# M in three groups a batch, batch 2's scores in the fixed banks, and another order of loads at the start

## The chip, the cores and the metric

The kernel runs on one core of a Trainium2 chip. A core has TensorE (PE; its weight loads are shown as PEld), VectorE (DVE), ScalarE (ACT), GpSimd (POOL) and SyncE (SP, which issues DMAs), an on-chip memory SBUF of 128 partitions, and PSUM, eight banks in which TensorE leaves its results. The metric is the time of one launch on the device in microseconds (us), lower is better, as a median of several runs.

## The reference

An attention block, and a feed-forward block behind it. B = 8 batches, H = 8 heads, S = 512 rows, Ns = 32 state rows, D = 64; then 8 x (512 + 32) = 4,352 rows of 512 pass through two weights with an ELU in between. All in fp32.

```
scores = x @ state.T / 8 ;  a  = softmax(scores)      # (S, Ns) for each batch and head
xread  = a @ state                                    # (S, D)
scores2 = state @ x.T / 8 ; a2 = softmax(scores2)     # (Ns, S)
sread  = a2 @ x
x_all  = concat(xread, sread) -> (B * 544, 512)
out    = elu(x_all @ w_in) @ w_out                    # w_in 512 x 2048, w_out 2048 x 512
```

## The kernel before

**M.** For x's rows the first product and the read are merged: `xread @ w_in = a @ (state @ w_in)`. The kernel makes M = state @ w_in for each batch (256 state rows, one set of 32 for each head, by 2,048 columns) and multiplies it with the transposed softmax, so w_in itself is used only for M and for the state rows at the end. M is made in half chunks `hc` of 256 columns, eight a batch, with small matmuls of 64 rows and 32 columns of the array (`by_state`), which fill two banks. `make_m` issues one or two half chunks as one operation of TensorE, `copy_m` brings the two banks to SBUF on ScalarE, and `sum_m` makes four block sums on GpSimd, for Strassen's scheme (seven block products in place of eight).

**Stages of a batch.** From batch 2 on a batch has a first half, `batch`: four chunks of 512 columns of g = elu(a @ M), each of seven products `two` in two parts, which use two ordinary banks (`pa`, `pc`) and a fixed one (`pb`); and a second half, `ffn2` (`ffn2_1` for batch 1): g @ w_out by two nested Strassen levels. There, each of the second-level products `second[k]` has seven steps of four matmuls in two banks. The next batch's scores, softmax, block sums of the softmax (`sum_a`), first M groups and state read are woven into this second half. Before the change M comes in four groups a batch: half chunks (0, 1) and (2, 3) in the second half of the batch before, (4, 5) and (6, 7) between the chunks of `batch`. The half chunks of w_in come from a copy in DRAM (`w_in_mem`) by `fetch`, into three slots of `w_half` (slot `hc % 3`).

**The start.** `start` loads states, x of batches 0 and 1 and the weights. Weights are converted by ScalarE and VectorE after loading (`convert`, sixteen blocks of 1 MB: eight of w_in, eight of w_out). `w_step` converts a block of w_in and makes M from it for batches 0 and 1. At the end of `start` stand batch 0's second half and the scores of batch 2. The operations of the loads have a `rank`, which sets their order on the DMA queue. In the first 40 us, where TensorE is planned to have nothing to do, `fill` matmuls (shown at L1590) keep it busy.

**What sets the order.** All operations are first collected in a `Plan`. A list scheduler with a cost for each operation (`Plan.run`) then fixes each engine's order before the program is built: TensorE takes operations in the order they were written if they are ready, the others by due times worked back from TensorE's, GpSimd and the DMAs as given. It also gives out the eight PSUM banks. Two of them, 6 and 7, are `fixed`: an operation that opens one takes just this one, and from the first such operation on the others share the remaining six. Before the change each fixed bank is opened by a product that serves only this, `ident_ready` (L1137), after batch 0's second half; the scores of batches 3 to 7 reuse those banks, batch 2's scores take two ordinary ones. `Plan.behind(op)` makes all operations collected inside it, except GpSimd's, wait for `op`.

`m_to` says where M of each chunk lies:

```python
m_to = {0: m_sb[:, 0], 1: m_sb[:, 1], 2: s_buf, 3: m_sb[:, 0]}
```

`s_buf` is also the place of a Strassen operand (`o.s`) in the second half. Nearly all instructions are issued by one helper, so their line is L464 throughout, and they are told apart by their tiles: `ps<-w_half,kT` is an M group, `ps<-aT,m` and `ps<-aT,s` are chunks, `ps<-w_out,g`, `ps<-sec`, `ps<-t_w,s` and the like are steps of the second half, `ps<-o,kT` and `ps<-xr,kT` are scores.

Of the kernel before, what the change touches and what calls it, by code (L numbers as in the profile page):

```python
# [86 lines left out]
class Plan:  # L87
# [108 lines left out]
    def prepare(self):  # L196
        for op in self.ops:
            op.users = []
            op.turn = self.places.get(op.number, op.number)
        for op in self.ops:  # L200
            for d in op.deps:
                d.users.append(op)
        self.opening = {}
        self.closing = {}
        for b in self.banks:
            self.opening.setdefault(b.first, []).append(b)
            self.closing.setdefault(b.last, []).append(b)
        self.kept = {b.first: b.fixed for b in self.fixed}
        self.all_banks = min([op.number for op in self.kept], default=0)
# [29 lines left out]
    def run(self, until=0.0):  # L239
# [9 lines left out]
        fixed = set(self.kept.values())  # L249
# [9 lines left out]
        def bank_time(op):  # L259

            if op in self.kept:
                return min([t for t, i in banks if i == self.kept[op]], default=None)
# [45 lines left out]
        while len(done) < len(self.ops):  # L308
# [26 lines left out]
            if op in self.kept:  # L335
                banks = [b for b in banks if b[1] != self.kept[op]]
                if self.kept[op] in holder:
                    after.append((holder[self.kept[op]], op))
# [51 lines left out]
def kernel(  # L390
# [297 lines left out]

    def m_blocks(m):
# [26 lines left out]
    def sum_a():  # L716
# [3 lines left out]
        (V if 0 else Q).tensor_tensor(out=t1, in0=r12, in1=r11, op=ALU.subtract)  # L720
        (V if 0 else Q).tensor_tensor(out=t2, in0=r22, in1=t1, op=ALU.subtract)
        (V if 0 else Q).tensor_tensor(out=r12, in0=r22, in1=r12, op=ALU.subtract)
        (V if 0 else Q).tensor_tensor(out=t4, in0=r21, in1=t2, op=ALU.subtract)
# [36 lines left out]
    def softmax(b, to):  # L760
# [15 lines left out]
        line(b, total_t, 1.0, eps)  # L776
        V.reciprocal(out=total_t, in_=total_t)
        for g in range(G):
            (V if 0 & 2 and b > 1 or b in [] else Q).tensor_tensor(
# [161 lines left out]
    class Second:  # L941
# [39 lines left out]
        def steps(self, out, fresh=False, base=None):  # L981
# [3 lines left out]
            x, y = bank(), bank()  # L985
            steps = []

            def step(n, ps, a, b, first, last, h, c):
# [10 lines left out]
                )  # L999
                o, p = (x[:, h, c * P : (c + 1) * P] for x in (out, base or out))  # L1000
                if n not in (0, 2, 3, 6):
# [10 lines left out]
            for n, args in enumerate((  # L1012
                (x, a11, self.b11, True, False, 0, 0),
                (y, a12, self.b21, True, True, 0, 0),
                (x, s[2], t[2], False, False, 1, 0),
                (y, s[3], t[3], True, False, 1, 1),
                (x, s[1], t[1], False, False, 1, 1),
                (y, a22, t[4], False, True, 1, 0),
                (x, s[4], self.b22, False, True, 0, 1),
            )):  # L1020
                steps.append(lambda n=n, args=args: step(n, *args))
# [128 lines left out]
    def start():  # L1150
# [22 lines left out]
        load_states(0, 1, raw_s, (SP, ACT))  # L1173
        load_x(0, x_halves, (SP, ACT))
        blocks[0] = weight_block(0, 2)
        load_states(1, 2, raw_s[:, 1:], (SP,))
        load_x(1, x_1)
        read_block(1)
        read_block(2)
# [4 lines left out]
        def w_step(hc):  # L1184
            convert_block(hc)
# [16 lines left out]
        turn_x(x_halves, ob, 1)  # L1202
        scores(0, ob)
        softmax(0, a_sb)
        w_step(0)
        ffn1(0, 0, (0, 1), 0 & 1)
        turn_x(x_1, ob)
        scores(1, ob)
        softmax(1, aT1)
        ffn1(1, 0, (0, 1), 0 & 2)  # L1210
        w_step(1)
        ffn1(0, 0, (2, 3))
        ffn1(1, 0, (2, 3))
        for c in range(1, 4):
# [3 lines left out]
            if c < 2:  # L1218
                for b in range(2):
                    softmax_rows(b)  # L1220
# [39 lines left out]
        scores(2, xr)  # L1260
# [14 lines left out]
    def first_m(b, at=None):  # L1275
# [7 lines left out]
        fetch(3)  # L1283

    def ffn2(o, b):
# [4 lines left out]
        o.sum_1()  # L1290
        late = [plan.ops[-1]]
        if 0:
            second[1].sums(o.a11, spare + s_2[0][:1])
            steps = second[1].steps(c12, fresh=True)
# [6 lines left out]
        if nxt:  # L1301
            first_m(b + 1, 1)
            scores(b + 1, xr, [f.view() for f in fixed])
        else:
            turn_read()
        for f in steps[1:]:
            f()
        second[2].sums(o.a12, s_2[1] + spaces(a_sb))
        late.append(plan.ops[-1])
        for f in second[2].steps(c11, base=c12):  # L1310
            f()
        late.append(plan.ops[-1])
        second[4].sums(o.a22, s_2[0] + spare[:2])
        late.append(plan.ops[-1])
        for f in second[4].steps(c21, fresh=True):
            f()
        second[6].sums(o.s, s_2[1] + spaces(a_sb))
# [11 lines left out]
        def soft_next():  # L1329
            if nxt:  # L1330
                with plan.behind(late[4]):
# [23 lines left out]
        if nxt:  # L1355
            make_m(b + 1, 2, 3)
            copy_m(b + 1, 1, m_to[1])
            sum_m(m_to[1])
            state_read(b + 1)
# [4 lines left out]
    def ffn2_1(o, b, x1):  # L1364
# [31 lines left out]
        make_m(b + 1, 2, 3)  # L1396
        copy_m(b + 1, 1, m_to[1])
        sum_m(m_to[1])
        state_read(b + 1)
# [34 lines left out]
    def batch(b):  # L1434
        for hc in range(4, 7):
# [8 lines left out]
        p[1] = ffn1_chunk(b, 1, g_sb)  # L1444
        p[0][1]()
        make_m(b, 4, 5)
        fetch(7)
        copy_m(b, 2, m_to[2])
        sum_m(m_to[2])
        p[1][0]()  # L1450
        p[2] = ffn1_chunk(b, 2, g_sb)
        p[1][1]()
        make_m(b, 6, 7)
        copy_m(b, 3, m_to[3])
        sum_m(m_to[3])
# [124 lines left out]
    ident_ready(0)  # L1580
    ident_ready(1)
# [50 lines left out]
```

## Time and profile before

| | |
|---|---|
| median of 3 runs | 702.73 us (702.24 to 704.44) |
| the profiled execution, on the device | 704.65 us |
| its span, first to last instruction | 702.9 us |
| mean granted TensorE clock | 0.997 |
| ACT, POOL busy (share of the span) | 43%, 21% |
| moved by DMA | 78.55 MB, 112 GB/s on average |
| matmul records of M groups (`ps<-w_half,kT`) | 1024, of 5794 on TensorE |

A row of the timeline gives the start in us, the length, engine, line, operation, the tiles it writes and reads (out<-in), the shape, and how many instructions were merged into it; in brackets, the idle time before it and what ended it. Matmuls overlap in the pipeline, so the length of a row is longer than the time until the next can start; the distance of two starts is the better measure. Every fp32 matmul call leaves two records. A row of the windows gives a stretch, its length, and the busy time of each engine in it with the number of instructions, then the granted clock, the DMA share and GB/s.

### The profile page before, as it was taken

To read this page: it belongs to the slowest core of one execution; us is meant where nothing else is said; L and a number is where in the kernel's file an instruction comes from. 1 tells how busy PE (TensorE), PEld (TensorE's weight loads), DVE (VectorE), ACT (ScalarE), POOL (GpSimd) and SP (SyncE) were. 2 spreads that over 40 slices of the span, in tenths; PEclk is the share of its full clock that TensorE was granted. 3 is DMA by queue.
4 is the path that set the end of the run, shared out by engine and by line. 5 is a ranking of instruction groups with operands and counts; after the bars stand their busy time and mean duration, and the time that the engine had idled before them with its cause. 6 is when DMAs were issued, how large, how long until landed. Compare 5 with 4: busy or idle time off the path is not lost.

```text
span 702.9 us, 14562 instructions
## 1 busy us (share of the span) xinstructions
PE 692.8 (99%) x5794; PEld 591.0 (84%) x5794; DVE 563.8 (80%) x991; ACT 303.9 (43%) x628; POOL 144.2 (21%) x161
## 2 busy tenths in 40 slices
PE   8899999999999999999999999999999999999997
PEld 7544468889988998889988998899888997899996
DVE  4899999999649985899669985998589966997650
ACT  4899982011148122742176215712373227500530
POOL 1300000052211062303530181116220453000000
PEclk9999999999999999999999999999999999999999
DMA  8578774204262505740471417450565034200300
GB/s 213 189 261 274 239 249 73 61 31 120 71 140 92 121 11 152 171 115 8 120 182 56 95 29 194 108 122 14 153 165 121 1 120 152 61 1 31 121 8 23
DMA packets 111268, 78.55 MB, mean 112 GB/s; under 512 B 89184, under 2 KB 92768, under 8 KB 111200
## 3 DMA queue, kind: packets, MB, share of 16 engines
q1 hardware_dynamic: 108988, 77.06, 39.4%
q8 instruction: 46, 0.75, 0.4%
q10 hardware_dynamic: 2212, 0.56, 0.4%
q14 instruction: 22, 0.18, 0.1%
HBM read 61.34 MB, written 13.11 MB: 106 GB/s over the span
## 4 chain that ended last, share of the span: by engine, by line
PE 94%; ACT 2%; DMA 2%; DVE 1%; SPq 1%; issue 0%; ACTq 0%; DVEq 0%
PE ps L464 93%; DMA g<-in_x_dram 1%; DMA xe<-in_x_dram 1%; SPq L464 1%; DVE w_half L464 1%; ACT sec L464 1%; ACT w_half L464 0%; ACT t_w L464 0%; PE ps L1590 0%; ACT m L464 0%; DVE sec L464 0%; DVE t_w L464 0%; ACTq L464 0%; DVE g L464 0%; ACT g L464 0%
## 5 line engine op out<-in xcount | busy, mean ns | idle before, releaser
L464 PE MATMUL ps<-aT,m 128*128 128x256 f32 (+1 forms) x568 | 149.7, 407 | 0.4 <-ACT m L464 0.4
L464 PE MATMUL ps<-w_out,g 128*128 128x128 f32 (+1 forms) x864 | 144.2, 315 | 0.0
L464 PEld LDWEIGHTS ps<-w_out,g 128*128 128x128 f32 x864 | 126.1, 191 | 14.9 <-issue 4.2
L464 PEld LDWEIGHTS ps<-aT,m 128*128 128x128 f32 x568 | 104.8, 190 | 33.3 <-issue 15.1
L464 DVE TENSOR_TENSOR o<-o,ps 128x128 f32<-128x128 f32 (+2 forms) x239 | 68.8, 289 | 66.9 <-PE ps L464 66.2
L464 ACT COPY o<-ps 128x128 f32<-128x128 f32 (+2 forms) x70 | 23.2, 335 | 158.7 <-PE ps L464 152.7
L464 POOL TENSOR_TENSOR xr<-xr,small 128x512 f32<-128x512 f32 x24 | 30.9, 1306 | 290.5 <-PE ps L464 147.1
L464 POOL TENSOR_TENSOR m<-m 128x256 f32<-128x256 f32 x72 | 63.6, 907 | 52.0 <-ACT m L464 50.6
L464 PE MATMUL ps<-sec 128*128 128x128 f32 x560 | 74.1, 275 | 0.0
L464 PEld LDWEIGHTS ps<-sec 128*128 128x128 f32 x560 | 68.5, 192 | 0.7 <-issue 0.4
L464 PE MATMUL ps<-t_w,s 128*128 128x128 f32 (+1 forms) x432 | 64.9, 298 | 0.0
L464 ACT ACTIVATE xe<-ps 128x512 f32<-128x512 f32 x96 | 54.4, 599 | 20.4 <-PE ps L464 15.0
L464 PEld LDWEIGHTS ps<-t_w,s 128*128 128x128 f32 x432 | 58.6, 192 | 3.3 <-ACT m L464 0.8
L464 ACT COPY m<-ps 128x512 f32<-128x512 f32 (+1 forms) x56 | 26.8, 535 | 55.6 <-PE ps L464 55.6
L464 DVE TENSOR_TENSOR ps<-sec,ps 128x512 f32<-128x512 f32 (+1 forms) x52 | 34.6, 673 | 17.5 <-PE ps L464 15.4
L464 DVE SCALAR_TENSOR_TENSOR g<-xe,ps 128x512 f32<-128x512 f32 x66 | 43.3, 684 | 1.7 <-ACT xe L464 1.1
L464 ACT COPY ps<-ps 128x512 f32<-128x512 f32 (+1 forms) x28 | 15.1, 541 | 61.2 <-PE ps L464 61.2
L464 ACT COPY sec<-ps 128x512 f32<-128x512 f32 (+1 forms) x52 | 29.7, 571 | 26.6 <-PE ps L464 18.5
L464 PE MATMUL ps<-aT,s 128*128 128x256 f32 x168 | 41.0, 379 | 0.0
L464 ACT ACTIVATE xe<-xe 128x512 f32<-128x512 f32 x66 | 38.8, 636 | 0.4
L464 PE MATMUL ps<-w_half,kT 64*32 64x256 f32 x1024 | 35.8, 382 | 0.6 <-DVE w_half L464 0.4
L464 PEld LDWEIGHTS ps<-aT,s 128*128 128x128 f32 x168 | 31.8, 190 | 4.5 <-DVE ps L464 0.2
(151 smaller groups left out, 1146.5 us busy)
## 6 DMA issues: line engine op xcount, KB each, us to landing
w_half<-w_in_mem SPq DMA_DIRECT2D x54, 512.0 KB
t_w<-in_moe_w_out_dram SPq DMA_DIRECT2D x8, 1024.0 KB
t_w<-in_moe_w_in_dram SPq DMA_DIRECT2D x7, 1024.0 KB
out_dram<-o SPq DMA_DIRECT2D x14, 512.0 KB
xe<-in_x_dram SPq DMA_DIRECT2D x26, 256.0 KB
o<-in_x_dram SPq DMA_DIRECT2D x80, 64.0 KB
w_in_mem<-w_half SPq DMA_DIRECT2D x8, 512.0 KB
xr<-xr SPq DMA_DIRECT2D x96, 32.0 KB
```

The costliest lines, as they stand in the source:

```text
L464: ins = getattr(engine, name)(**named)
```

## The change

Six edits come together.

1. **Three groups of M.** `make_three(b, pair, one)` makes three half chunks as one operation on TensorE: the pair into two banks as before, the single one into two more. `copy_one` copies the single half chunk into its place in M. A batch now has the groups (0, 1), (2, 3, 4) and (6, 7, 5). The second stands where (2, 3) stood, with a dependence on the first step of the second-level product before it. The third stands where (4, 5) stood. The sums of chunk 2 and chunk 3 both follow it.
2. **Fetches.** `first_m` fetches half chunk 4 as well; `batch` begins with 5, 6, 7 in place of 4, 5, 6 and fetches nothing later.
3. **Batch 2's scores in the fixed banks.** They become the operation that opens banks 6 and 7, both at once, which `Plan` learns to handle; the two `ident_ready` products go.
4. **Order of loads at the start.** The first block of w_in is ranked ahead of batch 0's x, and the second block ahead of batch 1's x; the third comes last. The order of the other work there, written as a string now, stays as it was.
5. **VectorE in place of GpSimd.** The last product of the softmax (times the reciprocal of the sum) for batches 0 and 1, and the four sums of `sum_a` in every batch that has them.
6. **The next batch's softmax** in `ffn2` waits for `late[3]` (the last sum of `second[4]`) in place of `late[4]` (that of `second[6]`).

Other variants in the diff are switched off by constants (`if 0`, `via = 0`, `sl = 0`, `fm = 0`) and are cut here.

```diff
-        self.kept = {b.first: b.fixed for b in self.fixed}
+        self.kept = {}
+        for b in self.fixed:
+            self.kept.setdefault(b.first, []).append(b.fixed)
...
             if op in self.kept:
-                return min([t for t, i in banks if i == self.kept[op]], default=None)
+                free = [t for t, i in banks if i in self.kept[op]]
+                return max(free) if len(free) == len(self.kept[op]) else None
...
+    def make_three(b, pair, one):
+
+        c = pair[0] // 2
+        ps = st[b, "m", c] = [bank(), bank()]
+        half = st[b, "m", one] = [bank(), bank()]
+        calls = []
+        for hc in (*pair, one):
+            w, h = st["w", hc], hc % 2
+            calls.append(by_state(
+                b, half if hc == one else ps, [w[:, m] for m in range(NP)],
+                slice(0, 256) if hc == one else slice(h * 256, (h + 1) * 256), hc == one or h == 0,
+            ))
...
+            products(1.38, sum(calls, []), "make_m", "state")
+
+    def copy_one(b, hc, to):
+        for g in range(G):
+            A.copy(
+                out=to[:, g * 512 + hc % 2 * 256 :][:, :256], in_=st[b, "m", hc][g][:, :256],
+            )
+        g_of[b, hc // 2] = to
...
-        (V if 0 else Q).tensor_tensor(out=t1, in0=r12, in1=r11, op=ALU.subtract)
+        (V if 1 else Q).tensor_tensor(out=t1, in0=r12, in1=r11, op=ALU.subtract)
...
-            (V if 0 & 2 and b > 1 or b in [] else Q).tensor_tensor(
+            (V if 0 & 2 and b > 1 or b in [0, 1] else Q).tensor_tensor(
                 out=rows(g), in0=rows(g), in1=bc(tops(b, g)["total_t"], NS), op=ALU.mult
             )
...
-        load_states(0, 1, raw_s, (SP, ACT))
-        load_x(0, x_halves, (SP, ACT))
-        blocks[0] = weight_block(0, 2)
-        load_states(1, 2, raw_s[:, 1:], (SP,))
-        load_x(1, x_1)
-        read_block(1)
-        read_block(2)
+        q2 = (SP, ACT)
+        for what in 'swxtvyu':
+            if what == "s": load_states(0, 1, raw_s, q2)
+            if what == "x": load_x(0, x_halves, q2)
+            if what == "w": blocks[0] = weight_block(0, 2)
+            if what == "t": load_states(1, 2, raw_s[:, 1:], (SP,))
+            if what == "y": load_x(1, x_1)
+            if what == "v": read_block(1)
+            if what == "u": read_block(2)
...
-        scores(2, xr)
+        scores(2, xr, [f.view() for f in fixed] if 1 else None)
...
         fetch(2)
         fetch(3)
+        if 1: fetch(4)
+
+    def next_m(b):
...
+            before = [op for op in plan.ops if op.name == "second"][-7]
+            make_three(b, (2, 3), 4)
+            plan.ops[-1].deps.add(before)
...
+        copy_m(b, 1, m_to[1])
+        if 1: copy_one(b, 4, m_to[2])
+        sum_m(m_to[1])
+        if not 0:
+            state_read(b)
...
-                with plan.behind(late[4]):
+                with plan.behind(late[3]):
...
-        for hc in range(4, 7):
+        for hc in range(5, 8) if 1 else range(4, 7):
             fetch(hc)
...
+        def m_three():
+            make_three(b, (6, 7), 5)
+            copy_one(b, 5, m_to[2])
+            copy_m(b, 3, m_to[3])
+            sum_m(m_to[2])
+            sum_m(m_to[3])
...
+        mm = 3
         p[0][1]()
-        make_m(b, 4, 5)
-        fetch(7)
-        copy_m(b, 2, m_to[2])
-        sum_m(m_to[2])
+        if mm == 0: m_2()
+        if mm == 1: m_both()
+        if mm == 3: m_three()
         p[1][0]()
...
         p[1][1]()
-        make_m(b, 6, 7)
-        copy_m(b, 3, m_to[3])
-        sum_m(m_to[3])
+        if mm == 0: m_3()
...
-    ident_ready(0)
-    ident_ready(1)
+    if not 1:
+        ident_ready(0)
+        ident_ready(1)
     ffn2_1(o, 1, x1)
```

## The prediction

> **What bounds the kernel now.** I read the page's first row (busy time), then the chain that ended last, then the row of granted clock.
>
> ```profile
> PE 692.8 (99%) x5794; PEld 591.0 (84%) x5794; DVE 563.8 (80%) x991; ACT 303.9 (43%) x628; POOL 144.2 (21%) x161
> ...
> PE 94%; ACT 2%; DMA 2%; DVE 1%; SPq 1%; issue 0%; ACTq 0%; DVEq 0%
> ```
>
> TensorE is busy 99% of 702.9 us and is 94% of the chain. A modelled busy time proves little by itself, so I look at the distance between starts in the timeline, which is the rate at which work really leaves.
>
> ```profile
> 335.13 1.06 PE L464 MATMUL ps<-t_w,s 128*128 128x128 f32 x8
> 336.12 1.09 PE L464 MATMUL ps<-w_half,kT 64*32 64x256 f32 x32
> 337.14 1.16 PE L464 MATMUL ps<-w_out,g 128*128 128x128 f32 x8
> 338.14 1.06 PE L464 MATMUL ps<-sec 128*128 128x128 f32 x8
> 339.03 1.06 PE L464 MATMUL ps<-t_w,s 128*128 128x128 f32 x8
> ```
>
> A product of eight records (two for each matmul call) takes 0.89 us from start to start (338.14 to 339.03) wherever one follows another, in all batches. So from about 36 us on TensorE streams without holes, and **a microsecond less of its instructions is a microsecond less of time**, as long as its suppliers keep up. The exceptions are the edges of an M group (the 64*32 row): the product before it takes 0.99 (335.13 to 336.12), the one after it 1.00.
>
> **The M groups.** What has one group less? Groups of one, two and three half chunks all occur in the trace:
>
> ```profile
> 68.42 0.66 PE L464 MATMUL ps<-w_half,kT 64*32 64x256 f32 x16
> 69.01 5.42 PE L464 MATMUL ps<-aT,m 128*128 128x512 f32 x12
> ...
> 81.23 1.53 PE L464 MATMUL ps<-w_half,kT 64*32 64x256 f32 x48
> 82.68 7.13 PE L464 MATMUL ps<-aT,m 128*128 128x512 f32 x16
> ```
>
> Start to next start is 0.59 for one half chunk (x16), 1.02 for two (x32, above), 1.45 for three (x48): 0.15 fixed and 0.43 for each half chunk. With the edges, 0.10 and 0.11, a group costs 0.36 whatever it holds. The matmuls are as many as before, so each batch from 2 to 7 saves one 0.36: **6 x 0.36 = 2.1 us**.
>
> [...] The row: copies of M on ScalarE have a median of 586 ns at 128x512 and a shortest of 354 ns at 128x256, so a group of three needs 2 x 0.59 + 2 x 0.35 = 1.9 us of copies behind 1.45 of matmuls. It holds four banks, of the six that are not fixed. Six of the twelve new groups, one in each batch, stand between two chunks: two banks chunk 0, four M, none left for chunk 1. By the rule chunk 1 waits until the copies end: 1.9 + 0.2 of delay, less the 0.86 of chunk 0's last product, 1.2 us. The other six stand beside a second-level product that already holds its two banks for seven products; taking 1.2 there too gives 12 x 1.2 = +14 us. By the rows, M copies start 0.16 after a group ends (355.49 to 355.65, group at 354.47) with ScalarE idle for 0.49 before, a half bank is free 0.35 later, and chunk 1 needs one bank first and the second 0.86 later: 0. I take 0, nearer to that row, and keep both ends.
>
> **Hidden parts of the same edit.** Fetches stay eight a batch. 5, 6 and 7 must now all land before one group. SP's queue issues 16 moves of attention rows until 344.76 and then two fetches at 344.86; a third there is 9 us ahead of the place of the old group (354.47). If it stays where it is (356.42, behind two stores and four block loads) the group slips to the old last group's place (361.85), still ahead of chunk 2. Cost 0; without that cover up to some 5 us. Six pairs of sums on GpSimd run back to back (2.92 us each, 21% busy), before chunk 2's second product: 0. ScalarE has two more copies a batch, at 43% load: 0.
>
> **The two readiness products.**
>
> ```profile
> 160.61 1.95 PE L464 MATMUL ps<-w_out 128*128 128x128 f32 x16
> 162.39 1.95 PE L464 MATMUL ps<-t_w,s 128*128 128x128 f32 x16
> ```
>
> They read weights twice, feed nothing, and occupy 160.61 to 162.39: **1.8 us less**, same shape as what follows, so no edge goes. What is late next is VectorE: the sum read by TensorE's `sec` product at 165.30 runs at 162.36 for 0.69 and ends at 163.05. Slack 2.2 us, of which 1.8 is eaten. Batch 2's scores (at 138.76) now wait for banks 6 and 7 both; their result is first used at 197.76, so even 20 us of delay are covered: 0.
>
> **Sums of the attention on VectorE.** GpSimd loses 24 of 0.95 us; VectorE gets 24 of 128x256 at 0.42 (its nearest row with that shape), 1.7 us a batch, in this stage (columns: stretch, length, then busy time of PE, PEld, DVE, ACT, POOL):
>
> ```profile
> 331.00:337.00 6.00, 6.00 (x79) 5.49 (x77) 5.35 (x13) 0.67 (x3) 5.75 (x7) 1.00 0.06 15
> 337.00:343.00 6.00, 6.00 (x60) 5.86 (x53) 4.41 (x8) 1.07 (x2) 5.92 (x7) 1.00 0.20 53
> ```
>
> VectorE's idle 0.65 + 1.59 holds it. Below: no gain, since no TensorE wait there names GpSimd. Above: all of it delays the evacuations behind it on VectorE, 6 x 1.7 = 10 us. I take 0. Softmax tied to an earlier sum (`late[3]`): the same instructions one product earlier; 0, at most 0.3 each way for five batches.
>
> **The start.**
>
> ```profile
> 10.94 1.09 PE L464 MATMUL ps<-o,kT 64*32 64x512 f32 x16 [0.27 <-DVE o L464]
> ...
> 19.09 2.29 POOL L464 TENSOR_TENSOR sec<-sec 128x512 f32<-128x512 f32 x2 [2.96 <-DVE sec L464]
> ...
> 25.08 0.70 DVE L464 STREAM_TRANSPOSE aT<-sec 128x512 f32<-128x512 f32 x1
> ...
> 26.54 3.60 PE L464 MATMUL ps<-aT,m 128*128 128x512 f32 x8
> ...
> 29.97 1.05 PE L1590 MATMUL ps<-sec 128*128 128x128 f32 x8
> ...
> 35.45 3.70 PE L464 MATMUL ps<-aT,m 128*128 128x512 f32 x8 [0.36 <-ACT m L464]
> ```
>
> Block 0 is 1.05 MB; the DMA row moves 332 to 379 GB/s when weights go, so x comes up to 3.0 us later and scores start at 13.9, not 10.94. From the first transpose (12.11) to the reciprocal's end (19.01) is 6.9; then two products on VectorE (0.6 apart by its 128x512 rows) and two transposes (0.7) make 2.7 with nothing between, where now the second transpose ends at 25.78. Ready: 12.1 + 3.0 + 9.6 = 24.7, **1.1 earlier**; block 0's conversion, which M waited for at 25.21, fits into the wait for x. But batch 1's x comes behind block 1, 3.0 later; its softmax runs from 23.27 to 38.08 on a VectorE that is busy nearly throughout and gets 4 x 0.6 more. Head start (conversion of block 0 from about 8 instead of 11.45), 3, against 3.0 of later data and 2.4 of added work that only partly collide. I take **-0.5**, range -3 to +2.
>
> [...] The trace's longest TensorE gap between 15 and 20 us is under 1 us, yet the clock granted in 20 to 25 is 0.68, and batch 1's scores take 1.89 from start to start where batch 0's took 1.02. [...] by the row one more such window over 128x512 products costs up to 1.7, and one less gives back 0.9. I take 0.
>
> **Sum.** -2.1 - 1.8 - 0.5 = -4.4. On the profiled execution: span 702.9 to 698.5, its time 704.65 (1.75 around the span) to 700.2. The median of the runs shown is 702.73, 1.9 below that execution; I forecast the median: **698.3**.
>
> **Rivals.** (1) *The start gives more*: if VectorE's head start counts in full, the hole of 29.97 to 35.45 closes by half, -3 in place of -0.5: 695.8. For it: that hole waits for M, hence for block 1, which now comes 3 us earlier. Against: batch 1's later x. (2) *VectorE is the bound between 40 and 180 us*: it is 8.8 to 10 of every 10 us there. Then the 1.8 turn into waiting at the `sec` product, the start is lost too, and only the groups stay, with some 0.6 given back: 701.2. Against: TensorE waits for VectorE hardly anywhere now, and batch 2's softmax can be put off. (3) *Slower: bank starvation.* The four banks of a group of three stop TensorE at the next bank it opens, at both places of each batch. At 1.2 us for each of 12 groups: 702.7 - 3.9 + 14.4 = 713. It decides from 0.5 us a group on (6.0 / 12). For it: 2 + 4 = 6 banks exactly; against: the copies' prompt start. (4) *The group isn't merged*: M's half chunk waits for its fetch or banks and other products come between; then 2.1 is lost, 700.4, part of rival 2's range.
>
> **How the numbers follow.** 0.3% is 2.1 us, about what this measurement can tell. Forecast 0.60 (696.3 to 700.3, all faster); rival 1 0.15 (faster); rivals 2 and 4 0.18, one third faster; rival 3 0.07 (slower). Faster 0.81, same 0.12, slower 0.07. The range 695.0 to 701.6 leaves a tenth at each end.
>
> **What would show it.** Right: three 64*32 rows a batch, two of x48 with 1.45 to the next start, and products of 0.89 right after; no `ps<-w_out` row near 160; batch period 75.8 (260.32 to 336.12) down to 75.4. Wrong: TensorE rows that wait for ACT `m` or `s` behind an x48 row (rival 3), for DVE `sec` near 161 (rival 2), or the first 128x512 products later than 26.5.

## The result, and the profile after

| | before | after |
|---|---|---|
| median | 702.62 us (702.24 to 704.44, 4 runs) | 696.89 us (696.14 to 697.11, 4 runs) |
| the profiled execution, span | 702.9 us | 695.1 us |
| ratio, 95% interval | | 0.9912 (0.9893 to 0.993) |

The forecast was 698.3, range 695.0 to 701.6. The page of after, first its row of busy time, then the row of the chain that ended last:

```profile
PE 684.7 (98%) x5782; PEld 590.5 (85%) x5782; DVE 572.4 (82%) x1019; ACT 302.2 (43%) x640; POOL 112.7 (16%) x133
...
PE 90%; ACT 4%; DMA 4%; DVE 1%; issue 1%; ACTq 0%
```

TensorE is still the bound: its busy time went down by 8.1 us, the span by 7.8. VectorE's rose by 8.6 us, from 80 to 82%, and GpSimd's fell by 31.5. The helper's line is now L466. The timeline of after, TensorE alone, shows the second and, further down, the first M group of a batch (batch 3's group of three, batch 4's group of two):

```profile
254.95 1.53 PE L466 MATMUL ps<-w_half,kT 64*32 64x256 f32 x48
256.41 1.16 PE L466 MATMUL ps<-sec 128*128 128x128 f32 x8
257.40 1.06 PE L466 MATMUL ps<-t_w,s 128*128 128x128 f32 x8
...
301.29 1.09 PE L466 MATMUL ps<-w_half,kT 64*32 64x256 f32 x32
```

The x48 row takes 1.46 to the next start, the edge behind it 0.99 for a product of 0.89. The first group of a batch starts at 226.08, 301.29, 376.50 and 451.71: a period of **75.21**, where the same rows of before are 75.79 apart (231.44, 307.24, 383.03, 458.82).

Around 160 us, the same view:

```profile
156.67 1.95 PE L466 MATMUL ps<-t_w,s 128*128 128x128 f32 x16
158.55 1.09 PE L466 MATMUL ps<-xr,kT 64*32 64x512 f32 x16
```

No `ps<-w_out` row stands ahead of `ps<-t_w,s` any more; batch 2's scores run behind it.

**Where the 5.7 us came from.** The two traces can be laid side by side at rows that both have. But before's first profiled execution was granted a clock of only 0.68 in 20 to 25 us. A second profile of before (next section) has a span of 701.4 and no such stretch, so I count against that one. The two traces differ by 6.3 us, the medians by 5.7; the parts below are parts of the 6.3.

| row | before, second profile | after | lead, and what it gained since the row above |
|---|---|---|---|
| first `ps<-t_w,s` of 128x256 | 123.47 | 122.14 | 1.33 (start) |
| `ps<-t_w,s` of 128x128 x16 | 161.00 | 156.67 | 4.33: 1.78 from the readiness products, 1.22 is only lent, as batch 2's scores are still to come |
| first M group of batch 3 | 230.05 | 226.08 | 3.97: the loan is paid back, 0.86 was gained in batch 2 |
| first M group of batches 4 to 7 | 305.83, 381.63, 457.43, 533.22 | 301.29, 376.50, 451.71, 527.51 | 4.54, 5.13, 5.72, 5.71 |
| end of TensorE's work | 696.73 | 690.42 | 6.31 |

So: start 1.33, readiness products 1.78, and 3.20 in the six batches 2 to 7, one of which (up to the row at 527.51) gained nothing. From the distances of starts, the 3.20 are 2.16 for six groups less (6 x 0.36), 1.19 of short waits between the products of the chunks and 0.44 of two waits for VectorE's sums at 166.79 and 167.92, which before has and after has not, less 0.59 for a standstill that only after has (batch 6).

### The profile page after: what moved, and what is told of

Same layout as the page of the kernel before. It is cut to its first block, busy times and chain, and to the rows that moved or that the text cites. A ratio compares the mean times of both kernels' runs of the same rounds, so it can differ in the third digit from the quotient of the medians.

```text
span 695.1 us, 14567 instructions
## 1 busy us (share of the span) xinstructions
PE 684.7 (98%) x5782; PEld 590.5 (85%) x5782; DVE 572.4 (82%) x1019; ACT 302.2 (43%) x640; POOL 112.7 (16%) x133
## 4 chain that ended last, share of the span: by engine, by line
PE 90%; ACT 4%; DMA 4%; DVE 1%; issue 1%; ACTq 0%
PE ps L466 90%; ACT sec L466 2%; DMA xe<-in_x_dram 1%; DMA t_w<-in_moe_w_out_dram 1%; DMA g<-in_x_dram 1%; ACT t_w L466 1%; DVE w_half L466 0%; ACT o L466 0%; DVE t_w L466 0%; DVE sec L466 0%; ACT w_half L466 0%; ACTq L466 0%; ACT g L466 0%; ACT m L466 0%; ACT s L466 0%
## 5 line engine op out<-in xcount | busy, mean ns | idle before, releaser
L466 PE MATMUL ps<-aT,m 128*128 128x256 f32 (+1 forms) x568 | 147.9, 405 | 0.2
L466 PE MATMUL ps<-w_out,g 128*128 128x128 f32 (+1 forms) x864 | 144.2, 314 | 0.0
L466 PEld LDWEIGHTS ps<-w_out,g 128*128 128x128 f32 x864 | 126.3, 191 | 12.4 <-issue 4.2
L466 PEld LDWEIGHTS ps<-aT,m 128*128 128x128 f32 x568 | 106.2, 190 | 29.6 <-issue 14.1
L466 DVE TENSOR_TENSOR o<-o,ps 128x128 f32<-128x128 f32 (+2 forms) x239 | 67.3, 286 | 41.2 <-PE ps L466 40.5
L466 ACT COPY o<-ps 128x128 f32<-128x128 f32 (+2 forms) x70 | 23.1, 335 | 145.6 <-PE ps L466 139.6
L466 POOL TENSOR_TENSOR xr<-xr,small 128x512 f32<-128x512 f32 x24 | 30.0, 1271 | 335.1 <-DVE small L466 171.3
L466 PE MATMUL ps<-sec 128*128 128x128 f32 x560 | 74.8, 277 | 0.0
L466 PEld LDWEIGHTS ps<-sec 128*128 128x128 f32 x560 | 68.5, 192 | 4.0 <-DVE o L466 3.7
L466 POOL TENSOR_TENSOR m<-m 128x256 f32<-128x256 f32 x72 | 60.5, 861 | 27.1 <-ACT m L466 25.7
L466 PE MATMUL ps<-t_w,s 128*128 128x128 f32 (+1 forms) x432 | 64.5, 298 | 0.0
L466 ACT ACTIVATE xe<-ps 128x512 f32<-128x512 f32 x96 | 54.9, 602 | 19.4 <-PE ps L466 12.8
L466 PEld LDWEIGHTS ps<-t_w,s 128*128 128x128 f32 x432 | 58.6, 192 | 2.5
L466 ACT COPY m<-ps 128x512 f32<-128x512 f32 (+1 forms) x56 | 28.1, 540 | 61.0 <-PE ps L466 60.9
L466 DVE SCALAR_TENSOR_TENSOR g<-xe,ps 128x512 f32<-128x512 f32 x66 | 43.9, 682 | 9.8 <-DMA w_half<-w_in_mem 5.8
L466 DVE TENSOR_TENSOR ps<-sec,ps 128x512 f32<-128x512 f32 (+1 forms) x52 | 34.9, 671 | 14.1 <-ACT sec L466 7.2
L466 ACT COPY sec<-ps 128x512 f32<-128x512 f32 (+1 forms) x52 | 29.7, 571 | 28.6 <-PE ps L466 28.5
L466 PE MATMUL ps<-aT,s 128*128 128x256 f32 x168 | 41.2, 379 | 0.0
L466 ACT ACTIVATE xe<-xe 128x512 f32<-128x512 f32 x66 | 39.8, 636 | 0.7
L466 PEld LDWEIGHTS ps<-aT,s 128*128 128x128 f32 x168 | 31.9, 190 | 4.3
L466 PE MATMUL ps<-w_half,kT 64*32 64x256 f32 x1024 | 34.9, 381 | 0.7 <-DVE xe L466 0.4
L466 PE MATMUL ps<-sec,g 128*128 128x128 f32 (+1 forms) x252 | 31.5, 272 | 1.2 <-DMA g<-in_x_dram 1.2
```

The source lines that it names most:

```text
L466: ins = getattr(engine, name)(**named)
```

## The experiments

Ratios are to the kernel before. After's is 0.9912, uncertain by 0.0018, that is by some 1.3 us, so the traces decide on the parts, at the rows of the table above ("the row at 122" is the first `ps<-t_w,s` of 128x256).

### The kernel before once more

No edit.

> The kernel before once more, unchanged, with a new profile. Question: does the window of half clock at 19.74 us (granted clock 0.68 in 20 to 25 us, batch 1's scores 1.89 us from start to start) belong to this kernel or to that one execution? Theory A (it belongs to that execution alone): the clock is 1.0 in 20 to 25 us, batch 1's scores take 1.02 us, the first product of w_out starts at 94.5 to 95.0 instead of 96.52, and the span is 700.5 to 701.5. Theory B (it belongs to the kernel, because its products wait longer near 15 to 20 us): the window comes again, the scores take 1.9, the first product of w_out is at 96.5 and the span is 702.5 to 703.

Ratio 0.9995 (0.9986 to 1.0005), span 701.4. Theory A. The windows and the timeline of this second profile of before:

```profile
20.00:25.00 5.00, 4.74 (x120) 2.76 (x120) 4.91 (x9) 4.76 (x12) 1.84 (x3) 1.00 0.47 149
```

```profile
24.74 3.60 PE L464 MATMUL ps<-aT,m 128*128 128x512 f32 x8
28.17 1.05 PE L1590 MATMUL ps<-sec 128*128 128x128 f32 x8
...
37.19 7.03 PE L464 MATMUL ps<-s,g 128*128 128x512 f32 x16
```

The eighth figure, the granted clock, is 1.00, and batch 1's scores take 1.02 (20.29 to 21.31). The same program, in the same order, was once given half a clock for a while and once not. That execution's 1.4 us at the row near 122 (124.86 against 123.47) belong to no edit.

### Four groups again

```diff
-        if 1: fetch(4)
+        if 0: fetch(4)
...
-        if 1:
+        if 0:
             before = [op for op in plan.ops if op.name == "second"][-7]
             make_three(b, (2, 3), 4)
...
-        if 1: copy_one(b, 4, m_to[2])
+        if 0: copy_one(b, 4, m_to[2])
...
-        for hc in range(5, 8) if 1 else range(4, 7):
+        for hc in range(5, 8) if 0 else range(4, 7):
...
-        mm = 3
+        mm = 0
```

> The changed kernel with M again in four groups a batch (two of x48 become one x32 and two pairs as before; the fetches of w_in as before), all other edits kept. Theory A (a group costs what stands around it and the short wait behind a group of two, 0.22 us a batch): 6 x 0.58 = 3.5 us, less the one stall of 0.6 us in the changed kernel's trace: 2.9 us slower than the changed kernel, 699.8; batch period 75.8, with the waits of the product aT,m behind a group of two back. Theory B (the prediction: only the 0.36 of a group): 2.1 us slower, 699.0, batch period 75.57. Rival (bank starvation, which the groups of three would cause): not slower, or faster than 696.9.

Ratio 0.9969 (0.996 to 0.9979), some 4.0 us above the changed kernel. More than either theory: the batch periods are 75.95, 76.48, 76.20 and 75.92. The 0.36 a group are there, and waits on top that the profile names (timeline, TensorE):

```profile
366.75 1.13 PE L466 MATMUL ps<-aT,s 128*128 128x256 f32 x4 [0.39 <-DVE ps L466]
```

A chunk's product waits for VectorE's sum into PSUM (`ps<-sec,ps`), the end of a chain from an earlier product over a copy on ScalarE. The first profile of before has the same wait in small: the sum ends at 356.36, and the product that needs it starts at 356.50, 0.12 later than the pace of its neighbours. The same sum in before (first profile) and in after:

```profile
355.66 0.70 DVE L464 TENSOR_TENSOR ps<-sec,ps 128x512 f32<-128x512 f32 x1
```

```profile
350.46 0.69 DVE L466 TENSOR_TENSOR ps<-sec,ps 128x512 f32<-128x512 f32 x1 [1.28 <-ACT sec L466]
```

In after it ends at 351.15, and the product that needs it, the fifth behind the group at 347.22, starts at 352.23, so nothing waits. That is not the longer group's doing: the group stands at another place. TensorE's rows ahead of it in batch 3, in before (second profile) and in after:

```profile
266.31 3.62 PE L464 MATMUL ps<-aT,m 128*128 128x256 f32 x16
...
275.45 1.89 PE L464 MATMUL ps<-aT,m 128*128 128x256 f32 x8
277.28 1.09 PE L464 MATMUL ps<-w_half,kT 64*32 64x256 f32 x32
```

```profile
262.76 1.89 PE L466 MATMUL ps<-aT,m 128*128 128x256 f32 x8
...
270.18 1.89 PE L466 MATMUL ps<-aT,m 128*128 128x256 f32 x8
272.01 1.53 PE L466 MATMUL ps<-w_half,kT 64*32 64x256 f32 x48
```

In before six products of the chunks (four records each) are done when the group comes, in after four; the chain then runs behind other products. **The planner's new order around the groups took these waits away**, some 0.22 us a batch, and the orders of other runs bring others back.

### The groups alone

```diff
-        for what in 'swxtvyu':
+        for what in 'sxwtyvu':
...
-        scores(2, xr, [f.view() for f in fixed] if 1 else None)
+        scores(2, xr, [f.view() for f in fixed] if 0 else None)
...
-            (V if 0 & 2 and b > 1 or b in [0, 1] else Q).tensor_tensor(
+            (V if 0 & 2 and b > 1 or b in [] else Q).tensor_tensor(
...
-    if not 1:
+    if not 0:
         ident_ready(0)
```

> The kernel before with only the three groups of M (and what its plan needs for them: the attention's sums on VectorE, late[3]); start, scores and readiness products as before. Theory A (0.58 us a batch): batch period 75.2 as in the changed kernel against 75.8, six times 0.58 = 3.5 us after the start, ratio to the kernel before 0.995 if the start keeps its length. Theory B (the prediction's 0.36): batch period 75.4, 2.1 us, ratio 0.997. The planner orders the start anew; what it does there is read apart, at the first product of w_out.

The sums on VectorE and `late[3]` stay with the groups here. Ratio 1.0016 (1.0004 to 1.0029): slower than before. The row at 122 comes at 129.41 against 123.47, so the start lost 5.9; the batch periods are 75.41, 75.39, 75.22 and 75.31, 0.46 below before's on average, between the theories. The loss in the start is none of the groups' own work: in that stretch the kernel makes M for batches 0 and 1, one half chunk at a time, as before. A part of it is the clock: this profile was granted half of it from 11.2 to 18.0 us. The other part is the plan, as the next runs show.

### The readiness products, and batch 2's scores

Both undone (`scores(2, xr, None)` and the two products back), then the products alone, then the scores alone.

> The changed kernel with the two readiness products back ahead of batch 0's second level and batch 2's scores in the pool's banks again; all other edits kept. Theory A (TensorE streams, a microsecond of its work is a microsecond of time): +1.8 us, 698.7, and the lead over the kernel before at the end of batch 0 is smaller by the same 1.8. Rival (VectorE is the bound from 40 to 180 us, so the two products cost nothing there): 696.9, with a TensorE wait for VectorE gone where the products stand.

> The changed kernel with only the two readiness products back ahead of batch 0's second level; batch 2's scores stay in the fixed banks. Theory A (TensorE streams there): +1.8 us, ratio to the kernel before 0.994, and everything up to about 156 us as in the changed kernel. Rival (VectorE bounds that stretch): +0 to +0.3, ratio 0.991. If instead it costs some 9 us, as the run with both edits undone did, then the readiness products disturb the schedule, not the scores' banks.

> The changed kernel with only batch 2's scores back in the pool's banks; the readiness products stay out. In the run with both edits undone 6.6 us were lost by the end of the first level of batches 0 and 1, before the readiness products. Theory A (that loss comes from the scores: free of the fixed banks they are no longer bound to that place, and the planner, which orders all engines anew, ends on a worse order of the start): +5 to +7 us, ratio to the kernel before 0.999 to 1.001. Rival (it comes from the readiness products being in the plan): +0 to +1 us, ratio 0.991 to 0.993. The prediction's value for this edit was 0.

| undone | ratio, 95% interval | against after | the row at 122 |
|---|---|---|---|
| both | 1.004 (1.0027 to 1.0052) | +9.0 us | 127.17 |
| readiness products | 0.9935 (0.9917 to 0.9953) | +1.6 us | 121.95 |
| scores' banks (its output is wrong, see below) | 1.0002 (0.9992 to 1.0011) | +6.3 us | 129.94 |

The products alone, on TensorE's timeline:

```profile
163.38 1.06 PE L466 MATMUL ps<-sec 128*128 128x128 f32 x8
164.27 1.95 PE L466 MATMUL ps<-w_out 128*128 128x128 f32 x16
166.06 1.06 PE L466 MATMUL ps<-sec,s 128*128 128x128 f32 x8
```

They occupy 164.27 to 166.06. TensorE's order behind them differs only by swaps of a few products. That kernel is 0.19 ahead of after at the row at 122, and 1.59 behind at the next x48 row (196.66 against 195.07): **1.78 us, and no engine behind TensorE took any of it**.

The scores are the surprise. The run with the scores alone leaves something out: with neither the readiness products nor the scores to open banks 6 and 7, ScalarE's copies open them, and the output is wrong (relative error 0.118). In all runs with a right output a product opens them; no run looks into why. So this run's time is not that of a kernel one could use, and I rest on the run with both undone, whose output is right. The scores' edit changes the banks into which one operation of 1 us at 158 us writes, and with them the moment from which the others share six banks. With the pool's banks the stretch up to 122 us takes 5.0 us longer, 36 us ahead of that operation; that the readiness products are not the reason is shown by the run with them alone, whose row stays at 121.95. (The run with the wrong output loses 7.8 there, up to 1.7 of it from half clock for 3.4 us.) The planner sets due times backwards from the end of the plan and hands out banks forwards, so this one constraint gives another order of the start on all engines. In the run with both undone TensorE issues nine M groups ahead of 130 us in place of seven, and these take 12.5 us in place of 10.1.

### The two edits of the start

Both undone, then the order of loads alone, then the softmax products alone:

```diff
-        for what in 'swxtvyu':
+        for what in 'sxwtyvu':
...
-            (V if 0 & 2 and b > 1 or b in [0, 1] else Q).tensor_tensor(
+            (V if 0 & 2 and b > 1 or b in [] else Q).tensor_tensor(
```

> The changed kernel with the old start: x ahead of the first block of w_in, and the softmax products of batches 0 and 1 on GpSimd; all other edits kept. Theory A (the trace's lead of 2.7 us at the first product of w_out is 2.0 of half clock in one execution, and only 0.7 belongs to the edits): +0.7 us in the median, 697.6. Theory B (the lead belongs to the edits): +2.7 us, 699.6. The prediction's own value was +0.5, its rival's +3.

> The changed kernel with the old order of loads (x ahead of the first block of w_in) and the softmax products of batches 0 and 1 still on VectorE. With both undone the start lost 2.0 us by the first products of w_out. Theory A (the loads make it: block 1 is converted earlier, the products on VectorE only cost VectorE time): about +2 us at the first product of w_out, span 697 or above. Theory B (the products on VectorE make it: the softmax of batch 0 ends a GpSimd detour of 2.3 us earlier): +0 to +0.5 at that place.

> The changed kernel with the softmax products of batches 0 and 1 back on GpSimd, the new order of loads kept. Theory A (the loads make the gain): +0 to +0.5 us at the first product of w_out. Theory B (the products make it): about +2 us there, with the first 128x512 products at 27 us or later instead of 25.66. If both this and the run with the old loads lose about 2, each edit needs the other.

| undone | ratio, 95% interval | against after | the row at 122 |
|---|---|---|---|
| both | 0.9959 (0.9946 to 0.9973) | +3.3 us | 124.12 |
| order of loads | 1.0021 (1.0011 to 1.003) | +7.7 us | 128.42 |
| products on VectorE | 0.9974 (0.9965 to 0.9983) | +4.4 us | 127.66 (up to 1.7 of it from half clock at 43.3 to 46.7) |

Either edit alone is dearer to undo than both. That can't be what the edits cost; again the plan is another one each time. Of the 3.3 us for both, 2.0 are lost by the row at 122, and 1.2 by two standstills of the kind that "Fetches on another queue" is about (1.75, where after has 0.59). So one more run kept the plan: the four products are planned as VectorE's, with VectorE's cost and place, but issued on GpSimd, and every engine's order stays.

```diff
+    VQ = Engine(DVE, nc.gpsimd)
...
-            (V if 0 & 2 and b > 1 or b in [0, 1] else Q).tensor_tensor(
+            (VQ if b in [0, 1] else Q).tensor_tensor(
```

> The changed kernel, with the planner's order of every engine left exactly as it is, and only the four softmax products of batches 0 and 1 issued on GpSimd in place of VectorE. With the planner free to order anew, the same edit cost 4.4 us. Theory A (the edit itself costs a detour: two products of 1.15 us on GpSimd for two of 0.64 on VectorE, and two more hand-overs, in a softmax that the first 128x512 products wait for): +1.0 to +1.5 us, ratio to the kernel before 0.993, first 128x512 products at 26.7 to 27.2 instead of 25.66. Theory B (the 4.4 are the edit's own): ratio 0.997. Rival (TensorE has other work there): +0, ratio 0.991.

Ratio 0.9928 (0.9916 to 0.994), which overlaps after's interval; the row at 122 is 0.36 earlier than after's, and so is the row at 122 of the run of the next section, which has the same plan and the products on VectorE (121.78 and 121.85). By the trace: nothing. The timeline of this run, then that of after:

```profile
21.98 2.37 POOL L466 TENSOR_TENSOR sec<-sec 128x512 f32<-128x512 f32 x2 [3.25 <-DVE sec L466]
...
24.39 0.71 DVE L466 STREAM_TRANSPOSE aT<-sec 128x512 f32<-128x512 f32 x1 [0.30 <-POOL sec L466]
```

```profile
22.81 1.28 DVE L466 TENSOR_TENSOR sec<-sec 128x512 f32<-128x512 f32 x2
24.01 1.29 DVE L466 STREAM_TRANSPOSE aT<-sec 128x512 f32<-128x512 f32 x2
```

GpSimd starts 0.08 behind the reciprocal (which ends at 21.90), VectorE 0.47 behind it (22.34), as it has other work first; the second transpose ends 3.20 and 2.96 after the reciprocal. The edit saves 0.24 us of a chain, not the 2.3 us of the two rows on GpSimd, and TensorE feels none of it. Theory A, too, was too high.

### Twice the copies behind each group of three

```diff
+        twice.extend(plan.ops[-4:])
...
+            twice.extend(plan.ops[-4:])
...
         op.emit()
+        if op in twice: op.emit()
```

> The changed kernel with the planner's order left as it is, and each of the four copies of M behind every group of three issued twice (12 groups, the second copy writes the same values again): 1.7 us more of emptying PSUM behind each group. The rule on PSUM (four banks of a group of three stop TensorE until they are copied): about 1.7 us for each of 12 groups, +20 us, ratio to the kernel before above 1.01, with TensorE rows that wait for ScalarE behind each x48 row. The prediction's row (nothing needs these banks so soon): +0 to +1 us, ratio 0.991 to 0.993.

Ratio 1.0014 (1.0008 to 1.002), +7.2 us: neither. TensorE's, ScalarE's and GpSimd's rows of one batch, from its timeline:

```profile
349.69 1.53 PE L466 MATMUL ps<-w_half,kT 64*32 64x256 f32 x48
351.14 6.44 PE L466 MATMUL ps<-aT,m 128*128 128x256 f32 x28
351.30 1.52 ACT L466 COPY s<-ps 128x256 f32<-128x256 f32 x4 [0.91 <-PE ps L466]
...
353.20 1.22 ACT L466 COPY m<-ps 128x512 f32<-128x512 f32 x2
...
356.47 1.20 ACT L466 COPY m<-ps 128x512 f32<-128x512 f32 x2
...
357.75 2.40 POOL L466 TENSOR_TENSOR m<-m 128x256 f32<-128x256 f32 x3 [1.93 <-ACT m L466]
...
359.31 0.89 PE L466 MATMUL ps<-aT,m 128*128 128x256 f32 x3 [0.86 <-POOL m L466]
```

Behind the x48 row TensorE goes on at once, here and behind the other group of the batch: **its banks are not what it waits for, even with 3.9 us of copies** (1.52, 1.22 and 1.20). What is late is the end of the other path from the same copies. The last copy of M comes 1.6 us later after its group than in the changed kernel, GpSimd's four sums follow it, and the first product of chunk 2 that reads a sum comes about 1.0 us late, once in each of batches 3 to 7. In the changed kernel that path has some 0.7 us to spare. At the end of TensorE's work this profile is 8.4 us behind after's: 4.9 of it are these five waits, and 2.8 are waits of two groups of three for the data of their fetches (at 195 and 503 us).

### Fetches on another queue

In after's batch 6 the second group of three takes 2.05 in place of 1.46 (timeline, TensorE):

```profile
497.64 1.09 PE L466 MATMUL ps<-w_half,kT 64*32 64x256 f32 x32
499.09 0.67 PE L466 MATMUL ps<-w_half,kT 64*32 64x256 f32 x16 [0.35 <-DVE xe L466]
```

This is why that batch gained nothing. The fetches of 5, 6 and 7 had landed by 497.02, and the VectorE row named has nothing to do with the group. In the run with both edits of the start undone, the same group of batches 4 and 6 stands still for 0.9 us, and for batch 4 the profile names nothing:

```profile
351.26 1.06 PE L466 MATMUL ps<-w_half,kT 64*32 64x256 f32 x21 [0.29 <-issue]
```

What the three have in common is in the records of the queue that the page calls `q8 instruction`. Its 46 transfers in after make one for every 255 of TensorE's 11,722 records, so I take them for TensorE's instructions; in the median 251 records lie between two. Ahead of these three standstills it was 471, 479 and 456, as the transfer came only when the three fetches were nearly through (in after it started at 496.84). TensorE goes on at its record 8,641 in after, and at 5,825 and 8,641 in the other run, 1.36, 1.29 and 1.37 us after that transfer ended. The two places are 2,816 records apart, eleven times 256; from this and from the one for every 255 above I estimate 256 records a transfer. With places counted in steps of 256 from 8,641, every other transfer of after ends 5.75 us or more ahead of its place. In all fourteen profiles the next smallest is 1.71 us, in a group that was waiting for its data. In the other kernels' profiles three groups of three stopped for longer than 0.6 us within, and all went on as the data of their half chunk landed (w_half at 196.27, 501.49 and 504.69). The three standstills are in batches 4 and 6. The run with the products on GpSimd has the same TensorE program as after, instruction by instruction: no gap between two transfers above 404 records, and the same group takes its 1.46. So the fetches went to ScalarE's queue, where they need not stand behind SP's 16 moves (10.7 us of issues in after, from 479.19):

```diff
-    def fetch(hc):
+    def fetch(hc, queue=SP):
...
-        dma(w, w_in_mem[:, hc], tokens=((f"mem{hc}",), ()), kind="fetch")
+        dma(w, w_in_mem[:, hc], tokens=((f"mem{hc}",), ()), queue=queue, kind="fetch")
...
         for hc in range(5, 8) if 1 else range(4, 7):
-            fetch(hc)
+            fetch(hc, ACT)
```

> The changed kernel with fetches 5, 6 and 7 of a batch issued on ScalarE's queue, so that they need not stand behind the 16 moves of SP's queue. In the changed kernel they go out together 8 us ahead of the second group of three and end 0.5 to 0.7 us before it; in one batch of six the group then stood still for 0.6 us, while TensorE's own next page of instructions had been fetched late (471 of its instructions after the page before it, where 230 to 270 are usual). Theory A (the stall comes from these bunched transfers): no x48 group takes more than 1.5 us, no page is 450 instructions or more behind the one before; 0.6 us faster, ratio 0.990. Rival (they only collide elsewhere, or ScalarE's three issues of some 0.5 us delay its copies): same or slower, ratio 0.991 to 0.995.

Ratio 0.9994 (0.9979 to 1.001), +5.8 us. The first half of the theory holds: no gap above 332 records, and all x48 rows up to 499 us take 1.46. But the time is the rival's: up to 529 us the kernel falls back by 1.5 us against after, and by 5.7 more behind it. This isn't the price of the queue, though: the plan is another one here too. TensorE's order differs from after's from 190 us on, and the last group of three stands 31.0 us behind the one ahead of it (562.50, 593.51) in place of 17.1. What the other queue alone costs stays open. One stop, on TensorE's timeline:

```profile
569.93 1.54 PE L466 MATMUL ps<-xe,xr 128*32 128x64 f32 x58 [1.89 <-issue]
```

The profile names no releaser for it; one of the rows moved for that product landed at 569.7, so I read it as a late move, without a run that shows it. Half clock follows it, from 570.3 to 573.7, and takes up to 1.7 of the 5.7.

The other price of three bunched fetches can be seen in the run with the readiness products alone: there, the fetches took 8 us to land, and the group waited for the data itself, in one batch 0.48 ahead of its first and 0.58 ahead of its second half chunk.

No run was faster than the changed kernel.

## Why the prediction was right, step by step

The time and the range held, and so did the main idea, that TensorE streams and a microsecond off it is a microsecond off the time. By the steps, against the second profile of before:

| step | predicted | found |
|---|---|---|
| groups | -2.1 | -2.16 |
| waits around the groups | not reckoned | -1.19 at the chunks, -0.44 in batch 2 |
| PSUM's banks behind a group of three | 0 (+14 at the other end) | 0 |
| fetches 5, 6, 7 before one group; GpSimd's sums; ScalarE's copies | 0 | +0.59; 0; 0 |
| readiness products | -1.8 | -1.78 |
| batch 2's scores | 0 | bound up with the order of the start |
| sums on VectorE, `late[3]` | 0 | no wait in the trace; not tried alone |
| start | -0.5 (-3 to +2) | -1.33 |
| sum | -4.4 | -6.3 in the traces, -5.7 in the medians |

**Groups.** The 0.36 of a group is right and is in every batch, and the rows of x48 fell where they were forecast, so rival 4 (the group isn't merged) falls. Missing were the waits between the chunks' products, some 0.22 a batch in before, which the order of after does not have. I took TensorE's stream to be without holes; distances of starts in before's rows would have shown these. They are no fixed gain of a longer group: with other kernels' orders the whole step came to 0.46 a batch (groups alone) and 0.93 (four groups again). That the planner's new order took waits away and brought none was luck.

**PSUM's banks.** The +14 was an estimate for a chunk that waits for its bank until the 1.9 us of copies end. It has no ground here: no run shows TensorE waiting for these banks, not even behind twice the copies (3.9 us). The slack that does bound the copies is that of GpSimd's sums, about 0.7 us; I had put these sums at 0 without giving their slack. Rival 3 (bank starvation) falls with it.

**Fetches.** I named the cover (the group may slip by up to 5 us) and missed that the group can start in time and stop in the middle. It cost 0.59 in one batch of six.

**Readiness products.** Exact, and the next-late engine was rightly judged: VectorE's slack of 2.2 us held, and the lead of 1.33 at 122 us is carried through VectorE's busiest stretch unchanged. Two products further on, where I had not looked, before does wait for VectorE (the 0.44 in batch 2); in after's order these waits are gone. Rival 2 (VectorE is the bound there) falls.

**Start.** The direction was right, the size is half of rival 1's, and the reason I gave is wrong. I expected the first 128x512 products 1.1 earlier, and my 25.78 for before came from the execution with half clock. In the second profile of before they are at 24.74, in after at 25.66, so batch 0's softmax is *later*, with x behind block 0. What pays is the hole behind, the one rival 1 named. In before, the products at 24.74 end at 28.17, and it takes until 37.19 to get through M of the second half chunk and batch 1's turn; in after (timeline, TensorE) the next M comes at once:

```profile
25.66 1.98 PE L466 MATMUL ps<-aT,m 128*128 128x512 f32 x4
27.58 1.09 PE L466 MATMUL ps<-w_half,kT 64*32 64x256 f32 x32
28.76 5.42 PE L466 MATMUL ps<-aT,m 128*128 128x512 f32 x12
...
36.41 7.03 PE L466 MATMUL ps<-s,g 128*128 128x512 f32 x16
```

That is 0.78 of the 1.33. The rest comes from a second hole, in before (second profile) at 46.42, against my "from about 36 us on without holes":

```profile
46.42 1.49 PE L464 MATMUL ps<-w_half,kT 64*32 64x256 f32 x32 [0.60 <-ACT m L464]
...
54.91 1.10 PE L464 MATMUL ps<-g,xr 128*32 128x64 f32 x64
```

```profile
44.52 1.10 PE L466 MATMUL ps<-g,xr 128*32 128x64 f32 x64
45.55 1.49 PE L466 MATMUL ps<-w_half,kT 64*32 64x256 f32 x32
```

After fills it with the product `ps<-g,xr`, and its lead grows to 2.10 at the M groups at 63.00 and 60.90; stops at two later M groups give 0.77 of it back. So the -0.5 had the right sign for a reason that did not hold. The softmax products on VectorE, from which I had 0.7 and more of my 1.1, bring 0.24 on their own chain and nothing on TensorE's.

**The clock.** In before's first profile 0.68 was granted in 20 to 25 us with no gap as long as 1 us between 15 and 20 us, and in the second, with the same order, 1.00. Taking 0 for it was reasonable: one and the same program had it in one execution and not in the other (last section).

**Scores.** No product waits for the scores, as I had reckoned, but that says nothing of what the edit was worth. With the new loads, the old banks give a start 5.0 us longer, as long as the planner is left to itself. The change's parts don't add up: undone one by one, the groups, the readiness products, the loads and the softmax products cost 4.0, 1.6, 7.7 and 4.4 us, 17.7 in all, where the whole change is worth 5.7.

## What to carry to other kernels

- Where a planner orders the engines, undoing one edit measures another plan, not the edit. Keep the order and change only the engine or the count: the softmax products cost 4.4 us the one way and none the other.
- A group's fixed cost (0.36 us here) can be reckoned from rows of before. A merged group also changes the order around it and bunches the transfers ahead of it; here the new order was worth another 0.22 a batch, and the bunched fetches lost 0.59 in one batch.
- When copies are delayed, look for what else reads them. PSUM's banks had room for 3.9 us of copies; the sums behind the same copies had room for 0.7.

## What the runs showed of the hardware that I had not expected

**TensorE stood still three times behind a late transfer of the instruction queue.** The page of after has its instruction queue:

```profile
q8 instruction: 46, 0.75, 0.5%
```

Its 46 transfers moved 0.75 MB, 16 KB each. All but one of after's ended 5.75 us or more ahead of the record that I count as theirs. The three that came late, one in after and two in the run with both edits of the start undone, stand behind a burst of data: with three transfers of 512 KB in flight they came some 200 records late (456 to 479 in place of 251), ahead of M groups that use up 96 records in 1.46 us, and these groups stood still for 0.6 to 0.9 us. That the late transfer is the cause is my reading; it rests on TensorE going on 1.29 to 1.37 us after its end at all three, at places that lie a multiple of 256 records apart, and on the comparison of equal programs. No run delayed such a transfer on purpose.

**Half clock came in one execution of a program and not in another.** Of the fourteen profiles here, five have half clock in mid kernel, in stretches of 3.41 us or twice that. In before's first profile it is 19.74 to 23.15 us, at a clock of 0.50, and the stretches of full clock on both sides are 13.65 and 679.25, that is 4 and 199 times 3.41. So I counted TensorE's busy share in steps of that length. Ahead of the half clock it was 0.62 in before (16.33 to 19.74 us) and 0.28 to 0.48 in the four others; but steps with 0.45 and 0.55 also occurred with full clock behind them. In these profiles TensorE was not idle ahead of the half clock, then, only thinly used, and no one share divides the two outcomes. The same program had half clock once and once not, at 1.4 us; what decides it is not shown by any run here.
